# Another order for all the work of a DeltaNet and gated-FFN kernel on one core

## The chip, the core and the metric

The kernel runs on one core of a Trainium2 chip. The core has five engines with instruction queues of their own: PE (matrix products, with the weight loads shown as PEld), DVE, ACT and POOL (elementwise work), and SP, which issues transfers; ACT and POOL can issue transfers too. Each engine takes its instructions in order and waits on semaphores. The metric is the device time of one execution in microseconds; before, it is 639.19 us, the median of three runs.

## The reference

Four batches of eight heads run a delta-rule recurrence over 768 steps with a head width of 48; the outcome, as 3072 tokens of 384 features, goes through a feed-forward block with h * cos(h) between two matrix products.

```python
k_n = k / (np.linalg.norm(k, axis=-1, keepdims=True) + 1e-06)
for t in range(S):                       # S = 768, per batch and head
    y[:, :, t] = np.einsum('bhd,bhde->bhe', q[:, :, t], state)
    v_old = np.einsum('bhde,bhd->bhe', state, kt)
    state = state + bt[:, :, :, None] * np.einsum('bhd,bhe->bhde', kt, vt - v_old)
...
x = attn_out.transpose(0, 2, 1, 3).reshape(3072, 384)
h = x @ w_in                             # 384 x 2048
out = (h * np.cos(h)) @ w_out            # 2048 x 384
```

## The kernel before

**The recurrence.** The 768 steps are cut into 24 units of 32 steps (`NU`, `C`). For each unit the kernel loads k, q and v, forms the norms of k (`square` on ACT, `sum` on DVE, `norms` on POOL, `scale` on DVE), transposes k and q (`turn` on PE, `turn_out`; from unit 8 on by transfers called `blocks`), forms the products of keys with keys and queries (`gram` on PE, `gram_keys` and `gram_queries` on DVE), and needs the inverse of a triangular matrix per head. For units 0 and 1 that inverse comes from repeated doubling: six levels of small products (`double`, line 757), each followed by copies on ACT (`double_copy`) and by transposes and sums on DVE (`double_turn`, `double_add`), in two halves per unit, the last number of a task's name. For every later pair of units m the keys' products go out to DRAM (`gram_put`), come back in another layout (`gram_get`), are inverted by a column loop on POOL (`inv`, lines 877 and 884), and go out and back again (`put`, `get`); only the first step `inv(1,0)` runs on DVE. Units 2 and 3 use two half-size inverses (`solve_half`, `between`, `solve`).

With the inverse there, the unit's serial part runs: `state` (line 928), `right`, `solve`, `solve_out` (line 1012), `update`, `update_out`, `within`, `within_out` (line 1068), `features` (line 1076), `features_out`. The next unit's `state` needs this unit's `update_out`.

**The feed-forward block.** Two units make one pair p of 256 tokens, twelve pairs in all. For pairs 0 and 1 the first product is plain: eight `hidden` tasks (line 1097). From pair 2 on it is a scheme with 20 block products (`layer`, line 1271) over sums of the inputs (`x_sum`) and of the weights (`in_sum`). The cosine gate follows (`turns`, `rest`, `cos`, `gate`). The second product is plain for pair 0 (`out`, line 1295) and a scheme of seven products for the others (`out`, line 1353, with `left` and `right` sums and `collect`); `store` writes the result. The weights come in 28 pieces (`weights`; 0 to 11 are `w_in`, 12 to 27 `w_out`), each converted by `split` on ACT, `shift` on DVE and `add` on POOL (line 538); a piece occupies one of eight large tiles, which the `ksq` tiles of `square` and the gates also use, until its `add`.

**Keep-warm products.** `keep_warm` (line 493) multiplies constants into a corner of PE's tile `p_out` that nobody reads. Five stand at the start (`WARM_FIRST`); the others are tasks in the order (`WARMS`). The function issues nothing once an `out` task has begun. The `scale` tasks of the first three pairs put their reciprocals into another corner of the same tile (`spare_out`, lines 589 to 596).

**What sets the order.** All work is a list of named tasks. The class `Order` holds two tables: `LINE`, the numbers of the tasks in the order in which they are emitted, which is also each engine's order; and `OTHER`, the tasks that take their second choice: a transfer goes to ACT's queue instead of SP's, a sum to DVE instead of POOL or the other way round. `Order.run` emits the tasks along `LINE` and hands out the tiles of each pool as their last users are emitted. Data dependences become semaphore waits. At the end every instruction is pinned behind its predecessor on its engine, so that nothing reorders them.

Of the kernel before, what the change touches and what calls it, by code (L numbers as in the profile page):

```python
# [59 lines left out]
class Order:  # L60

    OTHER = {
        ('gram_put', 2), ('q', 3), ('gram_get', 1), ('inv', 1, 0), ('put', 1), ('gram_put',
        4), ('gram_put', 5), ('v', 7), ('v', 8), ('v', 9), ('blocks', 11, 1), ('gram_put',
        11), ('put', 5), ('v', 13), ('put', 6), ('gram_put', 15), ('gram_get', 7), ('get',
        15), ('v', 16), ('blocks', 16, 0), ('blocks', 16, 1), ('gram_put', 16), ('blocks',
        18, 1), ('k', 19), ('blocks', 19, 0), ('gram_get', 9), ('get', 19), ('gram_put',
        20), ('v', 21), ('gram_put', 21), ('put', 10), ('gram_put', 22), ('v', 23),
        ('gram_put', 23), ('gram_get', 11), ('right', 4, 4), ('left', 1, 1, 0), ('left', 1,
        3, 0), ('left', 1, 3, 1), ('store', 1, 0), ('x_sum', 2, 'd'), ('x_sum', 2, 'n'),  # L70
        ('x_sum', 2, 'm'), ('x_sum', 2, 'e'), ('x_sum', 2, 'k'), ('x_sum', 2, 'g'),
        ('x_sum', 2, 'i'), ('x_sum', 2, 'l'), ('x_sum', 2, 'f'), ('x_sum', 2, 'b0'),
        ('left', 2, 4, 1), ('left', 2, 3, 1), ('x_sum', 3, 'd'), ('x_sum', 3, 'n'),
        ('x_sum', 3, 'm'), ('x_sum', 3, 'e'), ('x_sum', 3, 'k'), ('x_sum', 3, 'g'),
        ('x_sum', 3, 'i'), ('x_sum', 3, 'l'), ('x_sum', 3, 'h'), ('x_sum', 3, 'b0'),
        ('left', 3, 4, 1), ('left', 3, 3, 1), ('x_sum', 4, 'd'), ('x_sum', 4, 'm'),
        ('x_sum', 4, 'g'), ('x_sum', 4, 'i'), ('left', 4, 3, 0), ('left', 4, 3, 1),
        ('store', 4, 0), ('x_sum', 5, 'd'), ('x_sum', 5, 'e'), ('x_sum', 5, 'l'), ('x_sum',
        5, 'h'), ('x_sum', 5, 'b0'), ('left', 5, 2, 0), ('left', 5, 4, 1), ('left', 5, 3,
        0), ('left', 5, 3, 1), ('store', 5, 0), ('x_sum', 6, 'd'), ('x_sum', 6, 'g'),  # L80
        ('x_sum', 6, 'l'), ('x_sum', 6, 'f'), ('x_sum', 6, 'b0'), ('left', 6, 1, 0),
# [18 lines left out]
    WARM_FIRST, WARMS = 5, 56  # L100
# [1846 lines left out]
```

## Time and profile before

| | |
|---|---|
| times of the three runs | 640.6, 639.19, 638.9 us |
| span of the profiled execution | 636.6 us |
| PE busy in it | 619.2 us (97%) |
| DVE, POOL, ACT busy | 495.1, 435.8, 297.7 us |
| mean granted clock of PE | 0.991 |
| transfers | 50.37 MB, mean 79 GB/s |
| keep-warm products | 72 matmul records (each product leaves two) |

The profile gives the span, from the first instruction to the last; the execution's own time is not listed beside it, and the median of the runs is 2.59 us longer than the span. Times inside the span are in microseconds from its start. A row of the timeline has the start, the duration, the engine, the line, the operation, output and inputs, the tile shapes and a count; in brackets stand idle time before it and what ended that. Rows of busy time by stretch give for each engine its busy time and, in brackets, how many instructions began.

### The profile page before, as it was taken

The numbers are of one execution on the slowest core, as the hardware profiler recorded it, in microseconds if no ns is written. First come the engines' busy times: TensorE is split into PE (matmuls) and PEld (weight loads), VectorE is DVE, ScalarE is ACT, GpSimd is POOL, SyncE is SP. The second block draws the span as 40 slices with busy tenths as digits, with TensorE's granted clock in tenths as the row PEclk, the third lists the DMA queues.
The fourth block names the chain that finished last, engine by engine and source line by source line (L and its number), as shares of the span: only waits on it lengthen the run. The fifth ranks groups of instructions, "written<-read, shape, count | busy, mean of one in ns | idle before, by whom it ended". The sixth has DMA issues, their size and how long they took to land.

```text
span 636.6 us, 24189 instructions
## 1 busy us (share of the span) xinstructions
PE 619.2 (97%) x10176; PEld 576.2 (90%) x10176; DVE 495.1 (78%) x1030; ACT 297.7 (47%) x528; POOL 435.8 (68%) x780
## 2 busy tenths in 40 slices
PE   5999989999999999999999999999999999999997
PEld 4877877987899999999999999999999999999997
DVE  5776656779998999887898888888888776566682
ACT  3457556562423444643642644733643553545440
POOL 5247788678788788887789888886884883112241
PEclk8899999999999999999999999999999999999999
DMA  8978656563651555435435344333304102000001
GB/s 173 221 171 213 121 155 146 93 118 60 116 68 22 94 90 99 60 67 104 61 70 98 56 73 90 58 57 67 74 3 81 44 1 43 19 2 26 1 25 26
DMA packets 209381, 50.37 MB, mean 79 GB/s; under 512 B 200920, under 2 KB 204280, under 8 KB 209272
## 3 DMA queue, kind: packets, MB, share of 16 engines
q1 hardware_dynamic: 161896, 35.03, 29.3%
q10 hardware_dynamic: 47072, 13.25, 10.0%
q8 instruction: 80, 1.31, 0.9%
q0 software_dynamic: 304, 0.54, 0.4%
q14 instruction: 29, 0.24, 0.1%
HBM read 38.55 MB, written 10.22 MB: 77 GB/s over the span
## 4 chain that ended last, share of the span: by engine, by line
PE 90%; DVE 3%; DMA 3%; ACT 1%; issue 1%; POOL 0%; SPq 0%; ACTq 0%; DVEq 0%
PE p_out L1353 29%; PE p_h L1271 27%; PE p_h L1097 6%; PE p_kq L928 4%; PE p_out L1295 3%; PE p_s L1025 3%; PE p_g L673 3%; PE p_h L757 3%; PE p_kq L1055 3%; PE p_u L1000 3%; PE p_out L493 2%; PE p_h L1353 2%; PE p_z L1076 1%; DMA kp<-in_k_dram 1%; PE p_t L640 1%
## 5 line engine op out<-in xcount | busy, mean ns | idle before, releaser
L877 POOL TENSOR_TENSOR part<-z,gb 128x126 f32<-128x126 f32 (+23 forms) x321 | 144.6, 451 | 46.7 <-DMA gb<-g_dr 21.2
L884 POOL TENSOR_TENSOR z<-z,part 128x126 f32<-128x126 f32 (+23 forms) x321 | 145.5, 453 | 25.1
L1353 PE MATMUL p_out<-w_out,g_ffn 128*128 128x192 f32 x672 | 121.9, 328 | 0.3 <-DVE o L1405 0.2
L1353 PEld LDWEIGHTS p_out<-w_out,g_ffn 128*128 128x128 f32 x672 | 107.7, 190 | 1.7 <-DVE o L1405 0.7
L1150 ACT ACTIVATE turns<-turns,halfpi 128x512 f32<-128x512 f32 x96 | 68.0, 719 | 55.7 <-DVE turns L1141 42.6
L1353 PE MATMUL p_out<-w_sum,g_ffn 128*128 128x192 f32 x496 | 89.7, 329 | 0.2 <-DVE o L1405 0.2
L1271 PE MATMUL p_h<-x_sum,w_in 128*128 128x128 f32 x640 | 84.0, 277 | 0.0
L1134 ACT ACTIVATE turns<-g_ffn,quarter_turn 128x512 int32<-128x512 f32 x70 | 49.8, 719 | 66.4 <-DVE g_ffn L1288 31.3
L1353 PEld LDWEIGHTS p_out<-w_sum,g_ffn 128*128 128x128 f32 x496 | 79.6, 190 | 1.2 <-issue 0.4
L1271 PEld LDWEIGHTS p_h<-x_sum,w_in 128*128 128x128 f32 x640 | 78.8, 192 | 1.1
L1288 DVE TENSOR_TENSOR g_ffn<-g_ffn,p_h 128x512 f32<-128x512 f32 x80 | 54.3, 681 | 17.3 <-PE p_h L1271 16.4
L1141 DVE SCALAR_TENSOR_TENSOR turns<-g_ffn,turns 128x512 f32<-128x512 f32 x70 | 55.3, 796 | 13.1 <-ACT turns L1134 13.0
L1068 ACT COPY y<-p_kq 32x384 f32<-32x384 f32 x96 | 45.2, 470 | 30.4 <-PE p_kq L1055 22.5
L1153 DVE TENSOR_TENSOR g_ffn<-turns,g_ffn 128x512 f32<-128x512 f32 x70 | 51.5, 745 | 3.8 <-ACT turns L1150 3.7
L1271 PE MATMUL p_h<-x_sum,in_sum 128*128 128x128 f32 x400 | 52.9, 277 | 0.0
L572 POOL TENSOR_TENSOR knrm<-ksum,halves 128x16 f32<-128x16 f32 (+1 forms) x14 | 36.4, 2602 | 23.9 <-DMA qp<-in_q_dram 12.6
L1271 PEld LDWEIGHTS p_h<-x_sum,in_sum 128*128 128x128 f32 x400 | 49.7, 192 | 0.8
L1405 DVE SCALAR_TENSOR_TENSOR o<-p_out,o 128x192 f32<-128x192 f32 x74 | 25.1, 351 | 28.4 <-PE p_out L1353 28.0
L1097 PE MATMUL p_h<-x_ffn,w_in 128*128 128x128 f32 x384 | 45.8, 277 | 0.0
L1097 PEld LDWEIGHTS p_h<-x_ffn,w_in 128*128 128x128 f32 x384 | 44.1, 192 | 1.2
L1271 PE MATMUL p_h<-x_ffn,w_in 128*128 128x128 f32 x320 | 42.4, 277 | 0.0
L1369 POOL TENSOR_TENSOR g_ffn<-g_ffn,g_ffn 128x512 f32<-128x512 f32 x18 | 25.8, 1442 | 22.5 <-PE p_out L1353 18.7
(168 smaller groups left out, 1071.3 us busy)
## 6 DMA issues: line engine op xcount, KB each, us to landing
g_ffn<-in_moe_w_in_dram SPq DMA_DIRECT2D x10, 512.0 KB
gb<-g_dr SPq DMA_DIRECT2D x14, 256.0 KB
vp<-in_v_dram SPq DMA_DIRECT2D x68, 48.0 KB
g_ffn<-in_moe_w_out_dram SPq DMA_DIRECT2D x8, 384.0 KB
g_ffn<-in_moe_w_out_dram ACTq DMA_DIRECT2D x8, 384.0 KB
kp<-in_k_dram SPq DMA_DIRECT2D x120, 24.0 KB
out_dram<-o SPq DMA_DIRECT2D x14, 192.0 KB
zt<-z_dr SPq DMA_DIRECT2D x72, 32.0 KB
```

Source lines behind the costliest of these rows:

```text
L572: nc.gpsimd.tensor_tensor(out=scales[m][2][:, part], in0=sums[m, part.start][:, 0:n], in1=halves[:, 0:n], op=ALU.pow,)
L877: eng.tensor_tensor(out=part, in0=z[:, 0:rows, j, None].to_broadcast(shape), in1=a[:, j, None, j + 1 :].to_broadcast(shape), op=ALU.mult,)
L884: eng.tensor_tensor(out=behind, in0=behind, in1=part, op=ALU.subtract)
L1068: nc.scalar.copy(by_parity(y[quarter(b)]), p_kq[quarter(b ^ 1), :, b % 2])
L1097: nc.tensor.matmul(p_h[:, i], w_in[:, t, (4 * k + i) * 128 : (4 * k + i + 1) * 128], xts[p][:, t, unit * 128 : (unit + 1) * 128], start=(i ...
L1134: nc.scalar.activation(turns[p, f], hidden_of(p, f), AF.Identity, bias=quarter_turn, scale=TURN)
L1141: nc.vector.scalar_tensor_tensor(out=r, in0=hidden_of(p, f), scalar=TURN, in1=t, op0=ALU.mult, op1=ALU.subtract,)
L1150: nc.scalar.activation(r, r, AF.Sin, bias=halfpi, scale=2.0 * math.pi)
L1153: nc.vector.tensor_tensor(out=place(p, f), in0=step_of(rests.pop((p, f)), f), in1=step_of(hidden_of(p, f), f), op=ALU.mult,)
L1271: nc.tensor.matmul(p_h[:, e], in_block(*w)[:, e], x_of(p, b), start=new and e == 0, stop=True, skip_group_check=True,)
L1288: nc.vector.tensor_tensor(out=part_of(p, to), in0=part_of(p, one), in1=part_of(p, two), op=op)
L1353: nc.tensor.matmul(p_o, left(p, part, a)[:, e % 4], right(e, b), start=(e == 0), stop=(e == FT // 2 - 1), skip_group_check=True,)
```

## The change

Only the tables of `Order` change. The tasks, their instructions, their dependences and their tiles' pools stay the same, except that 16 keep-warm tasks stand in the order where there were 56.

```diff
 class Order:
     OTHER = {
-        ('gram_put', 2), ('q', 3), ('gram_get', 1), ('inv', 1, 0), ('put', 1), ('gram_put',
-        4), ('gram_put', 5), ('v', 7), ('v', 8), ('v', 9), ('blocks', 11, 1), ('gram_put',
...
+        ('q', 2), ('inv', 1, 0), ('gram_put', 6), ('gram_put', 7), ('v', 8), ('blocks', 9, 1),
+        ('put', 4), ('get', 9), ('gram_put', 10), ('blocks', 11, 1), ('blocks', 12, 0),
...
-    WARM_FIRST, WARMS = 5, 56
+    WARM_FIRST, WARMS = 5, 16
     LINE = """
-0 1 66 2 70 2084 3 71 4 8 9 72 122 67 68 5 2085 123 69 127 73 128 124 65 75 125 80 76 77 2088 178 78
...
+0 1 2 26 27 28 5 29 3 2044 30 31 32 138 33 4 34 6 35 82 83 87 8 9 10 11 12 37 36 2048 139 88 84 38
...
```

The choice between POOL and DVE is the same for every task. ACT's queue has 54 transfer tasks before and 32 after, SP's 149 and 171. Written out by names, with W for a keep-warm task, PE's order at the beginning is:

```text
before: turn(0) W W gram(0) turn(1) double(0,0,*) gram(1) W double(0,1,0) double(1,0,0) W W
  double(0,1,1) double(1,1,0) W W W double(0,2,0) W W double(0,2,1) double(1,0,1) turn(2) W W
  double(1,1,1) turn(3) ... double(0,5,*) turn(4) W solve(0) ... features(0) state(1) turn(5)
  double(1,4,1) gram(4) hidden(0,0) double(1,5,*) W W solve(1) W update(1) within(1) gram(5) W
  hidden(0,2) features(1) state(2) turn(6) hidden(0,4) solve_half(2) W between(2) W solve(2)
  hidden(0,6) update(2) W within(2) gram(6) hidden(0,8) features(2) state(3) turn(7) hidden(0,10)
  solve_half(3) between(3) solve(3) out(0,0,0) W W W W W hidden(0,12) W update(3) within(3)
  hidden(0,14) out(0,0,1) features(3) ...
after: turn(0) gram(0) turn(1) W W W W W double(0,0,*) W W W gram(1) W W W double(1,0,1) turn(2)
  state(0) W double(0,1,*) double(1,1,1) double(0,2,1) W double(1,2,1) double(0,2,0) ...
  double(0,5,1) double(1,1,0) turn(4) double(1,5,1) solve(0) ... features(0) state(1) turn(5)
  double(1,5,0) hidden(0,0) solve(1) hidden(0,2) update(1) within(1) gram(4) hidden(0,4) gram(5)
  state(2) features(1) hidden(0,6) turn(6) hidden(0,8) solve_half(2) between(2) solve(2)
  hidden(0,10) update(2) within(2) out(0,0,0) features(2) state(3) gram(6) hidden(0,12)
  solve_half(3) between(3) solve(3) out(0,0,1) turn(7) out(0,0,2) update(3) within(3)
  hidden(0,14) gram(7) state(4) hidden(1,0) hidden(1,2) hidden(1,4) features(3) ...
```

DVE's first entries and the transfers around the first reads of the inverse (a star marks ACT's queue) are:

```text
DVE before: sum(0,0) beta sum(0,1) scale(0,0) gram_keys(0) double_first(0) scale(0,1)
  double_rest(0) double_turn(0,0,1) gram_queries(0) double_turn(0,0,0) gram_keys(1) ...
DVE after: sum(0,0) beta scale(0,0) gram_keys(0) gram_queries(0) double_first(0) sum(0,1)
  double_rest(0) scale(0,1) gram_keys(1) double_first(1) shift(0) double_turn(0,0,1) ...
transfers before: ... *gram_put(4) *weights(15) v(4) *put(1) q(6) *weights(16) *gram_put(5) get(2)
  gram_get(2) weights(17) *weights(18) v(5) weights(19) q(7) *weights(20) get(3) weights(21) k(8) k(9)
transfers after: ... q(6) weights(17) put(1) weights(18) v(3) gram_put(4) gram_put(5) get(2)
  gram_get(2) weights(19) weights(20) q(7) weights(21) k(8) weights(22) get(3) weights(23) k(9)
```

On POOL `half_tiles` moves ahead of `norms(0,1)`. `q(2)` goes to ACT's queue and `q(3)` to SP's; `v(0)` moves behind `q(3)`. In the later part of the order the tasks of the same units and pairs stand in slightly other places.

61 lines of the change are left out of this document (29 added, 32 removed), and 196 rows, old and new, of the table LINE.

## The prediction

> **What bounds the kernel now.** I read the page's first part, then busy time by stretch, cut where the trace changes character, and then the same stretches for the keep-warm products alone (line 493).
>
> ```profile
> span 636.6 us, 24189 instructions
> PE 619.2 (97%) x10176; PEld 576.2 (90%) x10176; DVE 495.1 (78%) x1030; ACT 297.7 (47%) x528; POOL 435.8 (68%) x780
> ...
> 0.00:5.20 5.20, 3.84 (x10) 2.85 (x10) 2.77 (x12) 0.00 (x0) 4.10 (x11) 1.00 0.70 132
> 5.20:59.05 53.85, 46.50 (x932) 37.43 (x932) 39.28 (x118) 28.76 (x58) 24.69 (x26) 0.90 0.87 198
> 59.05:112.00 52.95, 48.95 (x1203) 43.26 (x1198) 33.32 (x69) 32.49 (x64) 44.04 (x83) 1.00 0.63 146
> 112.00:633.00 521.00, 519.95 (x8039) 492.62 (x8038) 419.37 (x832) 236.41 (x408) 362.96 (x662) 1.00 0.34 60
> 633.00:636.60 3.60, 0.00 (x0) 0.00 (x0) 0.35 (x1) 0.00 (x0) 0.00 (x0) 0.87 0.11 27
> ...
> 5.20:59.05 53.85, 14.59 (x48) 8.10 (x48) 0.90 0.87 198
> 59.05:112.00 52.95, 4.63 (x14) 2.17 (x14) 1.00 0.63 146
> ```
>
> The columns are the stretch, its length, then busy time of PE, PEld, DVE, ACT and POOL, the granted clock, the DMA share and GB/s; the last two rows have line 493's PE and PEld alone. From 112 us to the last product PE is idle for 521.00 − 519.95 = 1.05 us. That stage cannot be shortened by an order, because PE has the same products in it. What an order can win lies before 112 us. Call dead time PE's idle time plus the products that nobody reads. It is 53.85 − 46.50 + 14.59 = 21.94 us from 5.20 to 59.05 (the first FFN product begins at 59.05) and 52.95 − 48.95 + 4.63 = 8.63 us from there to 112. The question is how much of these 30.6 us the new order fills with FFN products, and what it adds later.
>
> **The change part by part.** The sum is made against the execution with the span of 636.6; the median of the runs, 639.19, lies 2.59 us above it, and I keep that difference.
>
> *Fewer keep-warm products.* A call of line 493 issues nothing once an output product has begun, so of the 56 tasks of before only the 31 ahead of `out(0,0,0)` do anything; with the 5 that stand first these are the 36 calls of x10 + x48 + x14 = 72 records. After, all 16 tasks issue: 15 calls go, not 40. They filled waits, so their leaving gains only what other work takes in their place.
>
> *PE's order.* The gain is read from milestones: whatever real work the new order has placed ahead of a milestone, less the time by which the milestone comes later. Rows of PE's timeline:
>
> ```profile
> 59.05 2.94 PE L1097 MATMUL p_h<-x_ffn,w_in 128*128 128x128 f32 x24
> ...
> 69.87 2.84 PE L1097 MATMUL p_h<-x_ffn,w_in 128*128 128x128 f32 x24
> 78.35 0.88 PE L958 MATMUL p_w<-rhs,w_sum 32*32 32x48 f32 x64
> 94.29 0.65 PE L640 MATMUL p_t<-consts,kp 128*128 128x128 f32 x4
> 94.78 0.60 PE L640 MATMUL p_t<-consts,qp 128*128 128x128 f32 x4
> 97.99 0.88 PE L958 MATMUL p_w<-rhs,w_sum 32*32 32x48 f32 x64
> 101.95 2.85 PE L1295 MATMUL p_out<-w_out,g_ffn 128*128 128x384 f32 x8
> 114.40 0.49 PE L1076 MATMUL p_z<-consts,y 128*128 128x128 f32 x3
> 114.83 1.15 PE L928 MATMUL p_kq<-st,kq_t 48*64 48x48 f32 x64
> 115.90 0.86 PE L673 MATMUL p_g<-kq_t 48*32 48x64 f32 x64
> ```
>
> These are, among others, `solve_half(2)` at 78.35, `solve_half(3)` at 97.99 and `features(3)` at 114.40. Setting the two lists side by side by task names:
> - ahead of `solve_half(2)` the new order has the same tasks and `hidden(0,6)` and `hidden(0,8)`: 2 × 2.84 = 5.7 us;
> - ahead of `solve_half(3)` it has `hidden(0,12)` and `out(0,0,0)` more and `turn(7)` less: 2.84 + 2.85 − 1.25 = 4.4 us;
> - ahead of `features(3)` it has `gram(7)`, `state(4)`, three `hidden` of the second pair and `out(0,0,2)` more: 0.86 + 1.15 + 8.5 + 2.85 = 13.4 us.
>
> *When the milestones come.* The waits are set by the inverse of units 2 and 3: POOL finishes it, `put(1)` writes it, `get(2)` and `get(3)` read it back.
>
> ```profile
> 63.62 0.35 POOL L884 TENSOR_TENSOR z<-z,part 128x15 f32<-128x15 f32 x1
> 65.01 0.37 ACTq L889 DMA_DIRECT2D z_dr<-z  x1
> 68.38 6.50 SPq L900 DMA_DIRECT2D w_sum<-z_dr  x8
> 74.97 1.75 SPq L852 DMA_DIRECT2D gb<-g_dr  x2
> ...
> 80.09 7.18 SPq L396 DMA_DIRECT2D qp<-in_q_dram  x4
> 87.31 4.57 SPq L900 DMA_DIRECT2D w_sum<-z_dr  x8
> 91.99 0.36 SPq L516 DMA_DIRECT2D g_ffn<-in_moe_w_out_dram  x1
> 92.45 9.47 SPq L396 DMA_DIRECT2D kp<-in_k_dram  x16
> ```
>
> Here lies the price of the change. ACT's queue has 54 DMA tasks before and 32 after; the rest go to SP. `put(1)`, `gram_put(4)` and `gram_put(5)` leave ACT and now stand on SP ahead of `get(2)`, with `v(3)`. SP issues in order, so `put(1)` holds it until POOL's last step (63.97 before; I take 65, since the first inverse step on DVE has one more doubling sum ahead of it). Then `gram_put(5)` must wait for `gram(5)`, which now stands behind `hidden(0,4)`, about 70. So `get(2)` runs from about 70.5 to 77 and has landed near 79. Behind the waiting SP stand the loads of `w_out` from `weights(18)` on, and behind those POOL's conversions. `solve_half(2)` comes at 79 against 78.35: gain 5.7 − 0.65 = 5.0.
>
> `get(3)` gets `k(8)` (half of 9.47), two or three weight loads (0.36 each) and the q load in front: 77 + 1.75 + 0.7 + q + 0.4 + 4.7 + 0.4 + 4.6, with q between 1.75, the nearest short group of transfers above, and the 7.18 that it took. This ends between 91.3 and 96.7, landed by about 93 to 98.5. PE's own work reaches `solve_half(3)` at about 95. So it comes at 95 to 98.5 against 97.99: a gain of 4.4 + 3.0 to 4.4 − 0.5, that is 3.9 to 7.4. From there to `features(3)` before takes 114.40 − 97.99 = 16.4 us; with the added 13.4 less the 4.4 already counted, 25.4, it comes at 120.4 to 123.9, and the gain there is 13.4 − 6.0 to 9.5, again 3.9 to 7.4.
>
> *The first 48 us.* The doubling of units 0 and 1 is a chain over PE, ACT and DVE with DVE busiest.
>
> ```profile
> L589 DVEq EVENT_SEMAPHORE  x4: 21/21/21, 11.0 to 55.4; - x4
> ...
> 8.70:48.28 39.58, 34.91 (x654) 28.24 (x656) 31.05 (x91) 20.09 (x41) 16.32 (x14) 0.87 0.84 200
> ...
> 11.58 1.64 POOL L572 TENSOR_TENSOR knrm<-ksum,halves 128x8 f32<-128x8 f32 x1 [0.56 <-DVE p_out L589]
> 16.79 1.18 PE L673 MATMUL p_g<-kq_t 48*32 48x64 f32 x64
> 48.28 1.02 DVE L1012 TENSOR_TENSOR u<-p_u,bz 128x384 f32<-128x384 f32 x2 [1.31 <-PE p_u L1000]
> ```
>
> DVE is idle for 39.58 − 31.05 = 8.5 us until `solve_out(0)` at 48.28. The new order puts `gram_queries(0)` and `double_first(0)` ahead of `sum(0,1)`, so `norms(0,1)` starts near 15.5 instead of 11.58. `scale(0,1)` writes a corner of the tile that keep-warm products write (line 589 shows waits of its own), so warms 5 to 7 wait for it, about 18.3, and `gram(1)` behind them comes near 20 instead of 16.79. DVE waits for that about 5 us in all. Afterwards its list is dense, with perhaps 1.5 us of waits, and 0.8 us longer. So `solve_out(0)` comes at 48.28 − 8.5 + 6.5 + 0.8 = 47.1, about where it was. If the chain leaves DVE all of its old gaps besides these 5 us, it is 54, and every milestone comes 7 us later; if nothing more than the 5 us is lost, 45.6. I take the dense case: ahead of each doubling sum or transpose the new list has other work that is ready, three to five entries of units 0 and 1 and of the weights in turn.
>
> *The clock.* In these rows the columns are as in the first fence.
>
> ```profile
> 8.00:10.00 2.00, 0.37 (x34) 0.32 (x34) 1.29 (x2) 1.62 (x5) 0.66 (x1) 1.00 1.11 223
> 10.00:12.00 2.00, 1.93 (x60) 1.44 (x39) 1.39 (x6) 0.53 (x1) 1.44 (x2) 0.76 0.83 219
> ...
> 11.00:14.50 3.50, 0.93 (x6) 0.53 (x3) 3.23 (x11) 2.16 (x4) 2.88 (x6) 0.51 0.74 186
> 14.50:21.30 6.80, 6.42 (x124) 5.48 (x126) 6.13 (x18) 2.42 (x6) 0.08 (x1) 0.50 0.90 204
> 21.30:24.00 2.70, 2.70 (x40) 2.25 (x38) 2.28 (x6) 1.94 (x5) 0.00 (x0) 1.00 0.96 185
> ...
> 19.05 1.97 PE L757 MATMUL p_h<-in_sum 64*64 64x128 f32 x16
> 22.66 1.09 PE L757 MATMUL p_h<-in_sum 64*64 64x128 f32 x16
> ```
>
> The granted clock was 0.5 from 11 to 21.3 us, and the same doubling group took 1.97 there and 1.09 after. PE had only 0.93 us of work between 11.0 and 14.5. Five of the 16 warms now stand right there, behind `turn(1)`; if they lift the clock sooner, two such groups win 0.9 each. I book nothing, since DVE waits for `gram(1)` anyway. [...]
>
> *Later.* In 112 to 633 us, `x_sum` and `left` keep their engines and the leads of `features` over their readers stay alike. I book 0 to 1 us of new stalls; below nothing it cannot go by more than the 1.05 us. Sum: the middle of 3.9 and 7.4 is 5.6, less 0.6 for such stalls: 5.0. Span 631.6, time **634.2**.
>
> **The rivals.** A measurement of this kernel tells about 0.3% from no change, 1.9 us: 637.3 to 641.1.
> - *SP becomes the bound (slower).* Against `get(2)` and `get(3)` stand queue places that before were ACT's. If the group of loads ahead of each takes 7.18 instead of 1.75, both come 5.4 us later than booked, together 10.9, and the gain of 5.0 turns into a loss of 5.9: 645. It decides from 5 us of lateness in all. For it: DMA share 0.87 up to 59 us and the 7.18 row. Against it: only one such row stands in this stretch, and PE has FFN work placed ahead of the waits. Chance 0.30, with smaller losses, from 641 on, in it.
> - *The gain is given back in the doubling (no change).* Half to all of DVE's old gaps stay beside the 5 us: `solve_out(0)` at 50 to 54, in the middle 5 us later than booked, 634.2 + 5 = 639.2. For it: a chain whose every link waits for another engine. Against it: the ready work placed between the links. Chance 0.07.
> - *The clock falls a second time (no change).* A second 10.2 us at half clock among the doubling groups, five groups at 0.88 more each: 634.2 + 4.4 = 638.6. For it: 15 calls fewer and more idle PE. Against it: from 59 to 112 us PE idled 4.00 us at clock 1.00. [...] Chance 0.06.
>
> **How the numbers follow.** The forecast, a gain over 1.9 us, has 0.57: 630 to 637, for a further 4 us is won if `get(3)` comes early and the clock returns sooner. The two rivals without change share 0.13; slower has 0.30. The range from 630 to 645 leaves about 1 in 10 above and less below.
>
> **What would show it.** Right: line 493 with 42 records; the first FFN product between 54 and 58; `solve_half(2)` near 79 with PE busy before it, `features(3)` near 121; less than 2 us of PE idle after 125. Wrong: a wait of PE for `get(2)`, `get(3)` or a conversion of `w_out` of over 3 us, `solve_out(0)` after 50, the clock below 1 after 25 us, or PE idle by more than 3 us in the long stage.

## The result, and the profile after

The changed kernel takes 646.22 us (643.89 to 649.52, four runs) against 639.67 for the kernel before beside it: a ratio of 1.0106 [1.0073, 1.0139], about 1% slower. Four more runs in a later comparison gave 648.28 us, 1.0132 [1.0103, 1.0162]. The forecast of 634.2 us was wrong, in its sign too; the result lies above its range.

First the page's busy times and the windows of the same stretches as before (stretch, length, busy time of PE, PEld, DVE, ACT and POOL, granted clock, DMA share, GB/s), then the keep-warm products alone (now line 488; lines after the tables are five lower than before).

```profile
span 644.9 us, 24110 instructions
PE 618.9 (96%) x10146; PEld 575.8 (89%) x10146; DVE 492.3 (76%) x1030; ACT 296.8 (46%) x528; POOL 429.6 (67%) x780
```

```profile
5.20:59.05 53.85, 41.53 (x792) 33.51 (x793) 37.39 (x104) 27.62 (x55) 22.66 (x18) 0.94 0.79 183
59.05:112.00 52.95, 49.01 (x1206) 43.32 (x1202) 33.99 (x79) 31.42 (x62) 41.55 (x78) 0.97 0.64 144
112.00:641.30 529.30, 524.51 (x8149) 495.87 (x8148) 417.86 (x836) 237.79 (x413) 361.28 (x674) 1.00 0.35 61
...
5.20:59.05 53.85, 10.37 (x34) 6.23 (x33) 0.94 0.79 183
```

PE is busy for 618.9 us where it was 619.2, and idle for 26.0 us (span less busy) where it was 17.4. That is the whole difference of the spans, 8.3 us. But the equal busy time hides two changes: 30 keep-warm records are gone (23.1 us of line 493 before, 14.2 now), and the real products, whose results are read, take 8.6 us more. (These two executions differ by 8.3 us; the medians differ by 6.6.)

Much of that is seen in the clock: three late intervals at half clock, each of which costs about half its 3.4 us, some 5 us by estimate (the granted clock is 0.50 in them, and a doubling group of the kernel before took 1.97 us at 0.50 and 1.09 at 1.00). Where the rest lies I can't tell. The windows are cut at the places where the granted clock changes; the first two rows are the start:

```profile
10.93:14.35 3.42, 3.42 (x13) 2.74 (x12) 2.85 (x11) 1.07 (x2) 1.63 (x5) 0.50 0.97 231
14.35:17.76 3.41, 2.52 (x39) 1.95 (x37) 2.50 (x5) 1.31 (x3) 2.00 (x1) 1.00 0.82 201
...
45.07:48.48 3.41, 1.44 (x30) 1.24 (x32) 1.48 (x5) 0.50 (x1) 0.00 (x0) 1.00 0.00 0
48.48:51.90 3.42, 3.42 (x31) 2.76 (x28) 2.31 (x6) 0.88 (x3) 1.64 (x2) 0.50 0.38 44
...
86.03:89.44 3.41, 1.39 (x100) 1.10 (x87) 0.56 (x1) 0.02 (x1) 2.38 (x8) 1.00 1.06 282
89.44:92.85 3.41, 3.41 (x24) 3.37 (x17) 3.12 (x9) 1.38 (x3) 2.78 (x9) 0.50 0.80 154
...
120.16:123.57 3.41, 1.87 (x39) 1.69 (x31) 1.33 (x4) 1.46 (x3) 2.94 (x8) 1.00 0.86 202
123.57:126.99 3.42, 3.42 (x19) 3.42 (x18) 1.78 (x5) 1.09 (x3) 2.65 (x2) 0.50 0.80 116
```

The three late intervals stand each behind one in which PE was busy for only 1.4 to 1.9 of 3.4 us. All the edges lie on one grid: 48.48 to 89.44 is 12 times 3.413, to 123.57 another 10 times. The kernel before had half clock from 11.05 to 21.29 us, three intervals, and then only from 635.69 us on, behind its last product. At the start the changed kernel has one, from 10.93 to 14.35 us: behind the five keep-warm products the clock came back two intervals sooner. So these two executions have four such intervals against three, and mean clocks of .989 and .991; over the runs the clock of the changed kernel is lower than that of the one before by more (.988 and .984 in its two series, against .995).

In each of the three half-busy intervals lies a stall that the waits call "issue": PE waited for nothing that the profile shows. The waits of PE (total, times, longest), and PE's timeline around `solve(2)`:

```profile
PE p_g L668 <- issue: 3.0, 2, 1.7
...
PE p_out L488 <- DVE bz L591: 2.1, 1, 2.1
...
PE p_kq L923 <- issue: 1.5, 1, 1.5
...
PE p_u L989 <- issue: 1.3, 1, 1.3
...
PE p_out L1348 <- DVE o L1400: 1.2, 1, 1.2
```

```profile
83.77 1.18 PE L953 MATMUL p_w<-rhs,w_sum 32*32 32x48 f32 x64
85.51 0.88 PE L953 MATMUL p_v<-g_ffn,in_sum 32*32 32x48 f32 x64 [0.57 <-ACT g_ffn L965]
87.07 0.61 PE L989 MATMUL p_u<-g_ffn,w_sum 32*32 32x48 f32 x37 [0.68 <-DVE g_ffn L973]
89.03 0.53 PE L989 MATMUL p_u<-g_ffn,w_sum 32*32 32x48 f32 x27 [1.34 <-issue]
89.48 3.76 PE L1092 MATMUL p_h<-x_ffn,w_in 128*128 128x128 f32 x17
```

And the same place in the kernel before:

```profile
79.17 0.70 PE L493 MATMUL p_out<-o 128*128 128x256 f32 x2
79.89 0.88 PE L958 MATMUL p_v<-g_ffn,in_sum 32*32 32x48 f32 x64
80.70 0.70 PE L493 MATMUL p_out<-o 128*128 128x256 f32 x2
81.45 0.86 PE L994 MATMUL p_u<-g_ffn,w_sum 32*32 32x48 f32 x59
83.87 0.28 PE L994 MATMUL p_u<-g_ffn,w_sum 32*32 32x48 f32 x5 [1.56 <-issue]
84.08 2.94 PE L1097 MATMUL p_h<-x_ffn,w_in 128*128 128x128 f32 x24
```

Keep-warm products stood there in the two waits; the stall was there too, but it came alone and the clock held (1.00 from 79.36 to 89.60 us). In the changed kernel stall and waits add up to 2.6 us, and the 17 `hidden` products behind them take 3.76 us, where the 24 of the kernel before took 2.94.

A ledger by the prediction's own milestones (later by, less real work placed ahead) shows where the loss arose: at `solve_half(2)` +0.3 us of gain (83.77 against 78.35, with 5.7 more work done); at `solve_half(3)` −1.1 (103.44 against 97.99, 4.4); at `features(3)` −4.3 (132.07 against 114.40, 13.4); at the first product of `layer(2,18)` −4.9 (170.32 against 158.84, with two `out` and one `gram` more, 2 × 2.85 + 0.86 = 6.6); at the end −8.3. From `solve_half(2)` to `features(3)` that is 4.6 us: two half-clock intervals cost about 1.7 each by estimate, and the stalls 1.34 + 1.54 where 1.56 stood before. At the end the second `p_g` stall (1.3) and the 1.2 us wait for `o` are most of the last 3.4.

### The profile page after: what moved, and what is told of

It reads as the page before. It is cut to its first block, busy times and chain, and to the rows that moved or that the text cites. A ratio compares the mean times of both kernels' runs of the same rounds, so it can differ in the third digit from the quotient of the medians.

```text
span 644.9 us, 24110 instructions
## 1 busy us (share of the span) xinstructions
PE 618.9 (96%) x10146; PEld 575.8 (89%) x10146; DVE 492.3 (76%) x1030; ACT 296.8 (46%) x528; POOL 429.6 (67%) x780
## 3 DMA queue, kind: packets, MB, share of 16 engines
q8 instruction: 80, 1.31, 0.9%
## 4 chain that ended last, share of the span: by engine, by line
PE 81%; POOL 6%; DVE 6%; issue 3%; ACT 1%; DMA 1%; SPq 0%; ACTq 0%; POOLq 0%; DVEq 0%
PE p_out L1348 26%; PE p_h L1266 25%; PE p_h L1092 7%; PE p_kq L923 4%; PE p_out L1290 3%; PE p_g L668 3%; PE p_s L1020 3%; POOL part L872 2%; PE p_kq L1050 2%; PE p_u L995 2%; POOL z L879 2%; PE p_h L752 2%; PE p_h L1348 2%; PE p_z L1071 1%; DVE g_ffn L1283 1%
## 5 line engine op out<-in xcount | busy, mean ns | idle before, releaser
L872 POOL TENSOR_TENSOR part<-z,gb 128x126 f32<-128x126 f32 (+23 forms) x321 | 142.1, 443 | 36.4 <-DMA zt<-z_dr 4.1
L879 POOL TENSOR_TENSOR z<-z,part 128x126 f32<-128x126 f32 (+23 forms) x321 | 141.2, 440 | 25.1
L1266 PE MATMUL p_h<-x_sum,w_in 128*128 128x128 f32 x640 | 85.4, 279 | 0.4 <-ACT g_ffn L1280 0.2
L1148 DVE TENSOR_TENSOR g_ffn<-turns,g_ffn 128x512 f32<-128x512 f32 x70 | 55.6, 802 | 12.1 <-ACT turns L1145 11.9
L1136 DVE SCALAR_TENSOR_TENSOR turns<-g_ffn,turns 128x512 f32<-128x512 f32 x70 | 51.7, 745 | 9.1 <-ACT turns L1129 9.1
L1092 PE MATMUL p_h<-x_ffn,w_in 128*128 128x128 f32 x384 | 49.7, 290 | 0.1
L1092 PEld LDWEIGHTS p_h<-x_ffn,w_in 128*128 128x128 f32 x384 | 47.2, 203 | 1.0 <-issue 0.2
L567 POOL TENSOR_TENSOR knrm<-ksum,halves 128x16 f32<-128x16 f32 (+1 forms) x14 | 36.9, 2636 | 13.3 <-DVE ksum L555 8.5
L1266 PE MATMUL p_h<-x_ffn,w_in 128*128 128x128 f32 x320 | 42.6, 277 | 0.0
```

The source lines that it names most:

```text
L567: nc.gpsimd.tensor_tensor(out=scales[m][2][:, part], in0=sums[m, part.start][:, 0:n], in1=halves[:, 0:n], op=ALU.pow,)
L872: eng.tensor_tensor(out=part, in0=z[:, 0:rows, j, None].to_broadcast(shape), in1=a[:, j, None, j + 1 :].to_broadcast(shape), op=ALU.mult,)
L879: eng.tensor_tensor(out=behind, in0=behind, in1=part, op=ALU.subtract)
L1092: nc.tensor.matmul(p_h[:, i], w_in[:, t, (4 * k + i) * 128 : (4 * k + i + 1) * 128], xts[p][:, t, unit * 128 : (unit + 1) * 128], start=(i ...
L1136: nc.vector.scalar_tensor_tensor(out=r, in0=hidden_of(p, f), scalar=TURN, in1=t, op0=ALU.mult, op1=ALU.subtract,)
L1148: nc.vector.tensor_tensor(out=place(p, f), in0=step_of(rests.pop((p, f)), f), in1=step_of(hidden_of(p, f), f), op=ALU.mult,)
```

## The experiments

Theories: **start** (the doubling of units 0 and 1 became longer and all else follows), **queue** (SP's longer queue, the prediction's rival), **clock** (keep-warm products had kept waits short of what costs the clock) and, formed after the first batch, **position** (issue stalls belong to a count of instructions).

### Halves of the two orders

Three kernels take one order up to a task and the other after it; each part keeps its own choice of queues and its keep-warm tasks. The fourth has the new order with the queues of the one before.

```diff
 start_old_rest_new:    LINE = before[.. solve(0)]      + after[rest]
 start_new_rest_old:    LINE = after[.. solve(0)]       + before[rest]
 to_unit2_old_rest_new: LINE = before[.. solve_half(2)] + after[rest]
 new_order_old_queues:  LINE = after;  OTHER (transfers only) = before's
```

> The order of before up to solve(0) and, from there, the new order (22 keep-warm tasks). Start theory: the new order loses its time in the doubling of units 0 and 1 (solve(0) at 52.52 us against 47.09), and its later part is worth the FFN products placed ahead; then this kernel is faster than before, 635 to 639, with solve(0) near 47 and solve_half(2) near 79. Later theory: the loss comes from waits and half-clock windows after solve(0), where keep-warm products are missing; then 642 to 646 in spite of the old start. Queue theory: SP's longer queue holds the inverse back; then also above 642, with the first get(2) late by over 5 us against 68.38.

> The new order up to solve(0) and, from there, the order of before with its keep-warm tasks. Start theory: 644 to 647, since solve(0) comes 5.4 us late and PE has nothing to fill it. Later theory: within 2 us of before, 638 to 642. Queue theory: in between, since the early transfers up to solve(0) are the new ones.

> The order of before up to solve_half(2), then the new order (28 keep-warm tasks). If all of the loss lies before solve_half(2), this is 636 to 640. If the fetch stalls and the half clock after it count, or the long stage after 112 us is worse by itself, 641 to 645.

> The new order with the transfer queues of before (54 transfer tasks on ACT's queue instead of 32). Queue theory: 640 to 643, with get(2) issued by 72 us instead of 77.26. Start theory: no change within 2 us, 644 to 648, since solve(0) stays near 52.5.

Measured: 644.71 us, 1.0087 [1.0054, 1.0119]; 650.41, 1.0183 [1.0141, 1.0225]; 641.81, 1.0045 [1.0025, 1.0066]; 671.72, 1.0517 [1.0467, 1.0568]. The four came out as follows.

- *Old start, new rest.* Giving back the old start wins only 1.5 us (3.6 against the second series), so in this form the start doesn't explain the loss; the start theory had 635 to 639.
- *New start, old rest.* At 650.41 us it lies above every forecast. Its profiled execution (645.11 us) tells more: it has one half-clock interval, from 11.0 to 14.4 us, and a mean clock of .997, and yet it comes to `solve_half(2)` 6.6 us later than before (84.97 against 78.35) and ends 6.7 us later. With nothing placed ahead to fill it, the late start (an issue stall of 1.2 us and whatever the seam adds are in it) costs about as much as the whole change, without any loss of clock behind it. In the changed kernel the 5.7 us of work placed ahead of `solve_half(2)` pay for the late start up to there.
- *Old order to `solve_half(2)`.* 641.81 us lies in the range for a loss that arises partly behind that task.
- *New order, old queues.* It is far slower, with a single wait of 9.7 us in the long stage, so it can't say what SP's queue costs early on. Its `get(2)` was issued at 78.99 us, not by 72, and its `put(1)` at 75.41. In the changed kernel, too, it is the inverse that is late: `put(1)` stands at 71.44 us, 65.01 before, and PE waits for neither `get(2)` nor `get(3)`. That, and not the run's time, speaks against the queue theory in the form in which the prediction held it.

```profile
314.67 2.08 PE L1267 MATMUL p_h<-x_sum,w_in 128*128 128x128 f32 x8 [9.71 <-ACT p_h L1279]
```

The wait of 9.7 us suggests that order and queues are fitted to each other; the seams of such hybrids may cost something by themselves. Differences of one or two us between these hybrids are therefore weak evidence. Their profiles gave the next lead, though. The kernel with the old start had stalls of 2.35 and 1.80 us in rows of small products, and a mean clock of .986 in that execution; the one with the old order to `solve_half(2)` waited 1.9 us for `between(2)`, where the old order has a keep-warm call, and had half clock at 87 to 94 us.

### Keep-warm calls put in and taken out

```diff
 new_warms_back:           after, + warm behind gram(3), ahead of double(1,1,0), between(2), solve(2), update(2)
 old_late_warms_out:       before, - warms 20 to 30 (turn(4) to within(2))
 new_scale_warms_out:      after, - warms 5 to 7 (between double(0,0,1) and gram(1))
 past_unit2_old_rest_new:  LINE = before[.. update(2)] + after[rest]
```

> The changed order with five keep-warm calls put back, at full 10 products: one behind gram(3), one ahead of double(1,1,0), one each ahead of between(2), solve(2) and update(2). Clock theory: the half-clock stretches of the changed kernel (beginning at 48.5, 89.4 and 123.6 us, 3.4 us each, each worth about 1.7 us) follow a stretch with 1.5 to 2.3 us of idle TensorE; the calls fill the two waits of 0.57 and 0.68 us around between(2) and the 0.68 us ahead of double(1,1,0), so the stretch at 89.4 goes and that at 48.5 goes in some of the runs, the one at 123.6 stays; mean clock rises from .987 to .992 or more, and the median from 646.2 to 642 to 644.5. Rival, the vector engine's chain alone sets the time and a keep-warm call only stands in TensorE's way: 646 to 648.

> The order before without its eleven keep-warm calls 20 to 30, which stand between turn(4) and within(2). Clock theory: the 1.56 us stall at 82.3 is then joined by 1.2 to 1.3 us of waits around between(2), a half-clock stretch follows near 85 to 89, perhaps one near 47 to 55; granted clock .985 to .992, median 640.5 to 645. Rival, the calls were TensorE time on the path (11 calls, 22 products of 0.35 us, 7.7 us): 632 to 638.

> The changed order without keep-warm calls 5 to 7, which wait for scale to leave the shared PSUM tile and stand ahead of gram(1); three calls, six products fewer. Position theory: the issue stalls come after a fixed number of instructions (596, 1477 and 2240 products in the changed kernel), so they move six products on: out of gram(3), which had 4 left, to about the second product of double(0,5,1); to 21 left of solve(2)'s p_u instead of 27; to 5 left of state(4)'s p_kq instead of 11. Rival, they belong to that work or to the transfers of that moment: they stay with the same products. Time: if the wait of 2.1 us for the shared tile is on the path, gram(1) and solve(0) come up to 2 us earlier and the median is 644 to 645; if the vector engine's chain sets solve(0), it is 645.5 to 647.

> The order before up to update(2), with its keep-warm calls 0 to 29, then the changed order; against the kernel that changed over at solve_half(2) (641.8, half clock at 87 to 94) it adds two calls around between(2) and the old order of what stands there. Clock theory: no half clock near 87 to 94, mean clock .995 or more, 638 to 640.5. Rival, the changed order's later work costs the 2.6 us: 641 to 642.5.

Measured: 645.02 us, 1.0096 [1.0074, 1.0118]; 640.26, 1.0024 [1.0005, 1.0042]; 645.63, 1.0118 [1.0090, 1.0147]; 642.30, 1.0058 [1.0039, 1.0077].

With the calls back, the profiled run had no half clock near 89 us, as the clock theory said, but the time fell by about 1 us, to 645.02 where 642 to 644.5 was said, and the mean clock hardly rose (.989 against .988, .992 was said): the interval at 47 stayed. Without the eleven late calls the old order lost the clock in two more places (49.1 to 52.5 and 66.2 to 69.6 us in its profile) and 0.24%: the loss that the clock theory called for, just under the lower edge of its range and at other places than the 85 us it named, and against the rival, for the calls did not cost time. `past_unit2_old_rest_new` is a miss: low clock near 87 to 94 gone and mean clock .9945, like the old order's .9946, but 642.3 us. So clock alone isn't it either: this is the range of the rival, by which the changed order's later work costs time itself.

What settled more is the third kernel, three calls or six products shorter ahead of the stalls. Windows from the start, for the changed kernel and then for this one, ending just ahead of a stall:

```profile
0.00:46.34 46.34, 34.30 (x596) 27.27 (x596) 30.31 (x91) 20.56 (x41) 18.80 (x24) 0.96 0.84 193
0.00:89.01 89.01, 72.79 (x1477) 62.06 (x1477) 61.37 (x165) 47.32 (x93) 49.59 (x68) 0.96 0.76 176
0.00:121.92 121.92, 102.72 (x2240) 86.62 (x2240) 79.52 (x203) 64.55 (x126) 76.48 (x129) 0.96 0.71 162
```

```profile
0.00:44.85 44.85, 34.00 (x596) 27.89 (x596) 30.66 (x92) 20.72 (x41) 18.80 (x24) 0.92 0.85 200
0.00:92.21 92.21, 74.85 (x1477) 65.13 (x1477) 61.24 (x165) 48.35 (x95) 50.76 (x72) 0.91 0.75 177
0.00:123.50 123.50, 104.40 (x2240) 89.42 (x2240) 79.21 (x204) 65.16 (x127) 75.53 (x125) 0.92 0.69 162
```

```profile
92.23 0.66 PE L986 MATMUL p_u<-g_ffn,w_sum 32*32 32x48 f32 x21 [2.20 <-issue]
123.52 0.32 PE L920 MATMUL p_kq<-st,kq_t 48*64 48x48 f32 x5 [0.36 <-issue]
```

The stalls come after the same 596, 1477 and 2240 products, while the work moved: 21 products of `solve(2)` were left instead of 27, 5 of `state(4)` instead of 11, and the first stall left `gram(3)`. Another, of 1.45 us, came after 1226 products, five blocks behind the first. They belong to a count of instructions, not to a task. The distances, 881 and 763, are 7 and 6 times 126 and 127. PE has a weight load for each product, so that is about 250 instructions; and the queues' list has 80 packets of 1.31 MB ÷ 80 = 16 KB for 10146 products, one for each 127. The second line is the same queue between 85.8 and 87.6 us:

```profile
q8 instruction: 80, 1.31, 0.9%
...
q8 instruction: 1, 0.02, 4.2%
```

The times of these packets bear on what PE waits for. Ahead of the three stalls one began at 43.90, 86.45 and 119.19 us, and PE went on at 46.36, 89.03 and 121.94, 2.5 to 2.8 us later; before, it was 80.98 and 83.87. In the traces of the two kernels every stall of PE that is called issue and lasts over 0.15 us, four and two of them, ended 2.4 to 2.9 us behind the start of such a packet. I take it from this that PE waits there for its next instructions; the profile itself names nothing. Counted from its own beginning, the block of 126 products that ends at 596 took from 41.8 to 46.36 us, that at 1477 from 84.5 to 89.03, that at 2240 from 117.5 to 121.94: 4.4 to 4.6 us each, however little of it was work. A block of as many `hidden` products would take 15 us by estimate (24 take 2.94 us). All six stalls stand among small products (`p_g`, `p_u`, `p_kq`); in other orders some stood ahead of large ones (1.53 us at 87.25 us in `old_late_warms_out`, 1.41 at 160.97 in `past_unit2_old_rest_new`). If these are blocks, the order decides which products share one.

As for time, the wait for the shared tile that this kernel was to remove stayed in part (1.5 us ahead of its keep-warm products), its clock was the lowest of these four (mean .983), and no gain can be told.

### Later seams, and 64 products ahead

```diff
 past_gram7_old_rest_new:  LINE = before[.. gram(7)]      + after[rest]
 past_long_old_rest_new:   LINE = before[.. layer(2,18)]  + after[rest]
 new_until_long_rest_old:  LINE = after[.. layer(2,18)]   + before[rest]
 new_shift64:              after, and behind the first five keep-warm calls
+    for _ in range(32):
+        nc.tensor.matmul(p_out[0:32, 0, 0:48], out_tiles[0][0:32, 0:32], out_tiles[0][0:32, 128:176])
```

> The order before up to gram(7), about 120 us, then the changed order. Place theory: what the changed order loses at full clock (640.6 at full clock when it begins after update(2), against 637.3 for the order before) is lost between 86 and 160 us, in waits for transfers and issue stalls; with the old order up to 120 us about half of it is gone: 638.5 to 640.5. Rival, it is lost in the long stage or at the end: 641 to 643.

> The order before up to layer(2,18), about 159 us, then the changed order. Place theory: nothing is left of the loss: 638 to 640, granted clock that of the order before. Rival, the changed order's long stage costs it (a 1.28 us issue stall at 431.9 us and a 1.20 us wait at 215.3 us stood there in the changed kernel): 640.5 to 643.

> The changed order up to layer(2,18), about 170 us, then the order before. Place theory: the whole loss stays: 645 to 648, with the three late half-clock stretches or as many of them as the changed kernel has. Rival, a quarter to a half of it lies in the long stage: 642 to 644.

> The changed order with 64 tiny products (32 calls of 32x32 by 48 columns into p_out, which the later keep-warm calls write over) behind the first five keep-warm calls, where TensorE waits for its first keys; the result is unchanged. Position theory: TensorE's instructions come in blocks of about 126 products, and a block that is worked off in less than about 4.4 us is followed by a stall up to that; the blocks now end 64 products earlier in the work, so the stalls inside gram(3), solve(2) and state(4) (1.70, 1.34 and 1.54 us in the changed kernel) go or shrink, a smaller one may come at 42.8 us and near 104 us; with them go the half-clock stretches that followed them; granted clock .990 or more, median 641.5 to 645. Rival, the stalls are bound to transfers or to those products: they stay, and the tiny products leave 646 or add up to 2 us.

Measured: 642.23 us, 1.0035 [1.0011, 1.0059]; 643.77, 1.0063 [1.0041, 1.0086]; 652.61, 1.0204 [1.0178, 1.0230]; 642.57, 1.0050 [1.0027, 1.0073].

The place theory missed all three, and the first came out as its rival said. Changing over later was no better (643.8 at 159 us against 642.2 at 120). The kernel with the old order to `layer(2,18)` comes there at 158.59 us, as before, and loses 4 us behind it: at the seam or in the changed order's long stage, which it can't tell apart. The third waits 8.1 us for `x_sum` at its seam and says nothing.

The 64 tiny products moved the stalls as the position theory said, and the time fell into its range, though they are 64 products more and put the first transposes off from 6.22 to 8.45 us. PE's timeline of that kernel at two of the three places, and the count ahead of the stall that is left:

```profile
0.00:44.64 44.64, 35.89 (x596) 29.46 (x597) 30.00 (x90) 19.40 (x40) 18.80 (x24) 0.92 0.84 200
```

```profile
44.66 0.33 PE L754 MATMUL p_h<-in_sum 64*64 64x64 f32 x4 [1.53 <-issue]
...
85.80 0.88 PE L955 MATMUL p_v<-g_ffn,in_sum 32*32 32x48 f32 x64 [0.57 <-ACT g_ffn L967]
87.36 1.50 PE L991 MATMUL p_u<-g_ffn,w_sum 32*32 32x48 f32 x64 [0.68 <-DVE g_ffn L975]
```

The stalls in `gram(3)`, `solve(2)` and `state(4)` are gone; one after 596 products is there again, now in `double`, and one of 0.65 after 1985. The gain, 1.0106 and 1.0132 to 1.0050, is about 4 to 5 us. But the half clock, which was to go with the stalls, did not:

```profile
46.24:49.65 3.41, 2.73 (x25) 2.27 (x22) 2.85 (x8) 0.37 (x1) 0.26 (x1) 0.50 0.23 25
...
83.79:87.20 3.41, 1.96 (x128) 1.58 (x128) 1.39 (x4) 1.56 (x4) 2.96 (x3) 1.00 0.99 254
87.20:90.61 3.41, 3.25 (x72) 3.14 (x73) 1.79 (x5) 0.00 (x0) 2.49 (x10) 0.50 1.09 282
```

It stands again at 46.24 to 53.06 and 87.20 to 90.61 us, the second time behind waits alone, and the mean clock over the runs is .989 (.990 or more was said). What fell in the profiled execution is PE's idle time, from 26.0 to 20.8 us, and the stalls in it from 5.9 to 2.4.

### Is it the position, or a fuller start?

```diff
 after_again:                 after, unchanged
 new_shift32:                 after, range(16) in the loop above
 new_shift64_warms:           new_shift64 with the five calls of new_warms_back
 old_shift96:                 before, range(48)
 new_shift64_free:            after, WARM_FIRST 5 -> 2, range(35)
 new_shift64_free_scale_out:  the same, range(38), - warms 5 to 7
```

> The changed kernel itself once more, to stand beside the next three on one chip: 644 to 649, median 646.2, granted clock .986 to .989; issue stalls after 596, 1477 and 2240 products as before, if they belong to a count of instructions.

> The changed order with 32 tiny products (16 calls) behind the first five keep-warm calls; the result is unchanged. A control on the 64 (642.6): they stand at the same place and warm TensorE nearly as long. Position theory: blocks end 32 products earlier, which still leaves them inside gram(3) (36 left), solve(2) (59 left) and state(4) (43 left), with blocks of small products ahead of them: the three stalls stay at 596, 1477 and 2240 products with 1 to 1.7 us each, and the median at 645 to 647. Rival, the tiny products help by their work at the start alone: 642 to 643.5, as with 64.

> The changed order with the 64 tiny products and the five keep-warm calls behind gram(3), ahead of double(1,1,0), between(2), solve(2) and update(2). Both theories together, if their gains add (3.6 us of the one, 1.2 us of the other): 640.5 to 642.5, clock .990 or more. Rival, the calls gain nothing once the stalls are gone: 642 to 644.

> The order before with 96 tiny products (48 calls) behind the first five keep-warm calls; the result is unchanged. Position theory: the block that ended inside solve(2)'s p_u (1.56 us of stall, 5 products left) then ends 96 products earlier, ahead of it, and the next among the hidden layer's large products: that stall goes; one of up to 1.7 us may come near 88 us. 636.5 to 639.5 against 639.2. Rival, tiny products at the start only delay the first keys' work: 640 to 642.

> The changed order with the same shift of 64 products, made without holding up the start: 35 tiny calls (70 products) take the place of three of the five first keep-warm calls (6 products), while TensorE waits for its first keys; the result is unchanged. In the kernel with 64 tiny products behind all five calls the first transposes came at 8.45 us instead of 6.22. Position theory: the stalls inside gram(3), solve(2) and state(4) are gone as there, and the start is up to 2.2 us earlier: 640 to 642.6. Rival, what the 64 tiny products won was a fuller start: 643 to 647.

> The same with 38 tiny calls, and without keep-warm calls 5 to 7, so that the shift is again 64 products behind gram(1), and gram(1) no longer stands behind a wait for the shared PSUM tile. If that wait is on the path once the stalls are gone: 638.5 to 641.5; if the vector engine's chain sets solve(0) regardless, as the kernel that left out the three calls alone said (645.6 against 646.2): the same as the kernel beside it within 1 us, or more where the clock falls for want of the calls.

| kernel | median us | ratio to before | mean clock |
|---|---|---|---|
| after_again | 648.28 | 1.0132 [1.0103, 1.0162] | .984 |
| new_shift32 | 645.36 | 1.0086 [1.0057, 1.0115] | .989 |
| new_shift64 (above) | 642.57 | 1.0050 [1.0027, 1.0073] | .989 |
| new_shift64_warms | 643.05 | 1.0056 [1.0032, 1.0080] | .990 |
| new_shift64_free | 642.39 | 1.0055 [1.0034, 1.0076] | .992 |
| new_shift64_free_scale_out | 641.88 | 1.0033 [1.0014, 1.0052] | .994 |
| old_shift96 | 642.28 | 1.0039 [1.0017, 1.0062] | .994 |

`after_again` has stalls after 596 (1.10 us), 1477 (1.46) and 7572 products (1.56, the fourth place of the first profile), one of 0.25 after 1985, and none after 2240, where one was expected. The count says where a stall can stand, not that it comes in every execution.

`new_shift32` is the control: half as many tiny products at the same place, a shift that leaves the block ends in the small products. In its timeline, and among its waits:

```profile
44.63 0.62 PE L670 MATMUL p_g<-kq_t 48*32 48x64 f32 x36 [0.42 <-issue]
86.92 1.49 PE L991 MATMUL p_u<-g_ffn,w_sum 32*32 32x48 f32 x59 [1.39 <-issue]
...
PE p_u L997 <- DMA zt<-z_dr: 2.9, 2, 1.5
```

36 and 59 products are left where 4 and 27 were, 32 more, as said; the stall in `solve(2)` is as long as ever, the first one shrank to 0.42, which was not expected, and the third didn't show. Its time lies between the two. The four kernels shifted by 64 are .33 to .56% over before instead of 1.06 and 1.32; their intervals lie below the second of the changed kernel's and overlap the lower edge of the first by .0007 at most. That the shift gains time is thus clear. That it gains it by the stalls is not shown: the control's interval overlaps all four, and in its profile the stalls are down to 1.8 us, fewer than with 64 (2.4), while PE idles 26.1 us as in the changed kernel, 2.9 of them in waits for transfers of `zt` that were 0.5 with 64.

`new_shift64_warms` didn't add the two gains, as its rival said: its calls moved later blocks by ten products, and stalls of 1.76 and 1.11 us appeared in `p_s` and `p_v`. A keep-warm call is itself a change of position. `new_shift64_free` failed at what its name says: the 70 tiny products took over 5 us, and the first transposes came at 9.07 us, later than with 64 behind the calls. The time was the same, so the gain is not due to an earlier start. `new_shift64_free_scale_out`, without the wait for the shared tile, is 0.5 us faster, within the noise: there is no sign that this wait decides the time. `old_shift96` missed its forecast. The stall in `solve(2)` went, as said, but in the profiled execution (647.37 us, the longest of twelve) two others came (0.78 and 0.99 us after 1607 and 1735 products), and the tiny products, at 80 ns each, put off the first transposes from 6.13 us to 13.71. None of these kernels beats the one before.

## Why the prediction was wrong

The step that failed is the choice in *The first 48 us*, "I take the dense case"; after it come two terms put at nothing, stalls for instructions and the clock behind 25 us. Between the span gain of 5.0 us that was booked and the 8.3 us lost in these two executions lie 13.3 us. By the ledger above 4.7 of them were gone at `solve_half(2)`, 4.6 went from there to `features(3)`, 0.6 to `layer(2,18)` and 3.4 behind it.

- *Fewer keep-warm products: right in count, wrong in what their place was worth.* 42 records, as said. "Their leaving gains only what other work takes in their place" held: over the whole execution nothing did. 8.9 us of them left and PE's idle time rose by 8.6.
- *PE's order: right.* The work placed ahead of the milestones was as listed.
- *The first 48 us: the term that failed first.* `gram(1)` came at 20.45 (near 20 was said) behind 2.09 us of waiting for `scale`. But then the dense case was taken, 6.5 us of idle DVE; measured in the window to `solve_out(0)` it was 44.90 − 32.89 = 12.0 us, and 53.85 instead of 47.1, the other end of the bounds (54) and past the 50 that was to show the step wrong. The waits of DVE in that window are shown below it.

```profile
8.95:53.85 44.90, 34.36 (x670) 27.86 (x670) 32.89 (x93) 21.21 (x43) 17.47 (x16) 0.92 0.73 177
```

```profile
DVE w_sum L680 <- PE p_g L668: 2.4, 1, 2.4
DVE w_sum L772 <- PE p_h L752: 2.4, 2, 1.5
DVE g L689 <- PE p_g L668: 1.9, 1, 1.9
DVE in_sum L768 <- ACT in_sum L760: 1.9, 1, 1.9
```

  The argument was that ready work stands between the links. It doesn't help a list that is worked off in order when PE or ACT is late: the 1.9 us for `in_sum` is an ACT copy, and 1.7 us of the wait for `p_g` at line 689 is the issue stall inside `gram(3)`. By the prediction's own rival this end alone gave no change, 639.2; the rest of the loss comes from the terms below.
- *When the milestones come: the waits right, the times late by the start.* `put(1)` was issued at 71.44 us (65 was taken), and so `get(2)` at 77.26 (70.5 was said) and `get(3)` at 95.51; PE waited for neither for more than 0.2 us. Here the rival that held .30, SP as the bound, had the right sign for a wrong reason.
- *The clock: booked at nothing.* Two of the three early half-clock intervals went, as the prediction thought possible, and three late ones came. The rival "falls a second time" had the event, a chance of .06, one place and no loss beside it; its 10.2 us were those of the kernel before (11.05 to 21.29 us) once more, and what came was three times 3.4 us. What that is worth can only be estimated: over the runs of all these kernels a common slope gives about 0.35 us for each .001 of mean clock, or 0.23 if one run of the kernel before at a clock of .945 (646.82 us) is counted with them. The changed kernel's .984 to .988 against .995 is then some 1.5 to 4 us of its 6.6 and 8.4. The new start with the old rest lost 6.7 us at a clock of .997, so the clock is not needed for a loss of this size.
- *Later: 0 to 1 us was said.* It lost another 3.4 us behind `layer(2,18)` and 0.6 ahead of it.
- *Not in the prediction at all: the issue stalls.* The trace of before had one, 1.56 us in `solve(2)`, and I took it for a fact of that place. They came to 5.9 us in the changed kernel against 2.1, and one stands in each interval ahead of a late half-clock one.

Shown by experiment: that the stalls sit at fixed counts (four lengths of the work ahead, from 6 fewer to 64 more products) and that the shift by 64 products gives back about half the loss or more. Shown in traces only: that each of the six stalls over 0.15 us in the two main traces ends 2.4 to 2.9 us behind the start of a packet of instructions, that the new start with the old rest, its seam included, is 6.6 us late at an undiminished clock behind 14.4 us, and that stalls and waits together precede the loss of the clock. Not shown: how the loss divides among the late start, the stalls and the clock, since seams and shifts move the block ends and the waits as well and no hybrid here isolates one of them; and by which of these the shift gains. Left open, too, is the remaining .33 to .56%, and why the clock fell behind some half-idle windows (1.54 us idle from 120.16 to 123.57) and not behind others (1.58 from 31.41 to 34.82).

## What to carry to other kernels

In long stretches of small products, find the stalls for which nothing is to blame and count the products ahead of them: here the counts stayed at 596, 1477 and 2240 when the work moved by six products, a packet of instructions began 2.5 to 2.8 us ahead of each stall's end, and 64 cheap products ahead moved the stalls out of `gram(3)`, `solve(2)` and `state(4)`; I read them as ends of blocks of instructions. Whether that gains time has to be measured: with 64 it did, with 96 in the other order it didn't. Products that nobody reads were part of the tuned order, both for the clock and for the position of all that follows: with eleven of their calls taken out of the order before, where they filled waits, two more half-clock intervals came and the time rose by 0.24%, and with three taken out of the changed order the stalls came six products later in the work. And a chain over three engines that are each worked off in order should be forecast with its waits left in, unless a trace shows that they close.

## What the runs showed of the hardware

- Queue q8, which the profile lists as instruction, moved 80 packets of 16 KB in either kernel (1.31 MB), one for about 127 of PE's products (10146 and 10176) with their weight loads. All six stalls that the waits call issue and that lasted over 0.15 us in the two traces ended 2.4 to 2.9 us after such a packet began. The blocks of 126 products ahead of the first three stalls of the changed kernel took 4.4 to 4.6 us, the one ahead of its fourth 3.4, and the two of the kernel before 4.4 and 3.1, so the 4.4 us that the position theory named are no fixed limit.
- In the two traces the granted clock changed between 1.00 and 0.50 only at edges of one grid of 3.413 us: before, at 11.05, 21.29 and, 180 steps on, 635.69 us; in the changed kernel at both ends of the intervals from 10.93, 48.48, 89.44 and 123.57 us, which is 33 steps from the first to the last. The interval from 120.16 us, with 1.54 us of idle time, was followed by one at half clock, that from 31.41, with 1.58, was not. In the kernel before, the 1.56 us stall was divided by an edge of the grid (21.30 + 18 × 3.413 = 82.73) and the clock held; that the edge is the reason is not shown:

```profile
79.36:82.77 3.41, 2.88 (x127) 1.88 (x127) 1.83 (x6) 1.91 (x4) 3.10 (x7) 1.00 1.04 260
82.77:86.18 3.41, 2.31 (x23) 2.24 (x23) 2.20 (x6) 1.75 (x4) 2.72 (x9) 1.00 0.73 210
86.18:89.60 3.42, 3.42 (x144) 2.78 (x144) 0.95 (x1) 1.85 (x5) 2.85 (x8) 1.00 0.39 96
```

  The grid stood differently in two executions of the changed kernel: half-clock intervals began at 48.48 us and, in `after_again`, at 47.69. Whether that is why its runs spread over 5.6 us (643.89 to 649.52) was not shown.
- Of the changed kernel's twelve `shift` operations on `w_in`, ten took 0.38 to 0.42 us on DVE; `shift(3)` took 1.42 at 27.03 us, beside a POOL addition in the same tile (26.88 to 28.16), and the one at 39.96 us took 0.88 beside another (39.27 to 40.56). One at 59.91 us took 0.42 though an addition began 0.16 us later. The reason is not shown.
